# Moving row additions, output copies and evictions by gaps between matrix products

## The chip, the core and the metric

The kernel runs on one core of one Trainium2 chip. The metric is the device time of one execution in microseconds (us); the comparison is by the median of several runs. The profile is of one execution of its own, so its span and its time differ a little from that median.

The engines that matter here are PE (matrix products), ACT and DVE (elementwise work), POOL (which in this kernel only issues DMAs) and SP (which only issues DMAs too). The program gives each of them one instruction stream.

## The reference, cut to what matters

Two results are computed from the same tokens (2048 of 576 values) and mixed by a gate for each token.

```python
def _A_ref(x, w_r, w_i):
    X = rfft2(x); X = X * (w_r + 1j * w_i); return irfft2(X, s=(S, D))
def _B_ref(x, w_gate, w_up, w_down):
    h = gelu(x @ w_gate) * (x @ w_up)          # 576 -> 4608, twice
    return h @ w_down                          # 4608 -> 576
g = sigmoid((x * gate_w).sum(-1, keepdims=True))
return g * _A_ref(x) + (1 - g) * _B_ref(x)
```

All data is float32. The products are made accurate by splitting each operand into a high and a low part and adding three products.

## The kernel before, in words

**The products set the frame.** After a short opening, the program goes through 34 blocks in `products(b, k)`, k from 0 to 33. A block makes seven combined products of gate and up (a Strassen scheme; the loop over n from 0 to 6) for 1024 tokens and two of the hidden tiles. Each of the seven has two halves, each half is one call of `seven` with seven matrix products of 512 columns. Between them stand the down products: `down` makes one with twelve products of 288 columns, which add up in one of two PSUM buffers `pdn`. A block has eight of them: three after n = 1, three after n = 4 and two after n = 6. The last block has two after each of the first five and `finale` makes the last eight in another way.

**The gap is the unit of order.** Nothing is scheduled by hand in time. Each `seven` and each `down` ends in one call of `gap`. A gap counts up `count[0]`, runs all functions that `at(n, fn)` has put off to this count (in the order of their due count, equal ones in the order in which they were put off), then runs the work of `post`, and gives the rest of its room to one generator of other work (`gens[0]`), which computes the spectral half. Note that `at(1, fn)` before a `gap` puts `fn` into that very gap, behind whatever was due there already. The program only fixes the order of each engine's stream; at run time engines wait by semaphores.

**Credit.** Each product adds its length times 1.08 to `credit[0]`; each DVE operation takes its cost from it. The generator runs while the credit is positive. What is carried over is held to `cap[0]`: 2.0, and 3.0 in the column stage. A generator that yields nothing ends its turn for this gap. A second generator in `side` runs beside it.

**The spectral half** goes forward over the rows, through the column stage (`columns`, 16 column products on PE from `product`, operands loaded by POOL), and back over the rows in two halves h = 0 and h = 1 (`inverse_rows(h)`). For h = 0 the last part is, in this order: `fetch(2)` loads a quarter from the DRAM array `home` into `tmp`; `adds` scales eight finished rows, each into one of five places (three in `wtb`, two in `low`), by DVE and ACT in turn, and two gaps later has POOL add it to `yd[u]` in DRAM by an accumulating DMA; `spin` (a butterfly of ten DVE operations) and `settle` (copies on ACT and DVE back to `rows`) treat the fetched quarter; then the last quarter is fetched into `tmp` (index 0 of `places_of`), and after seven gaps spun and settled. Index 1 of `places_of` means `wtb` and `low` in place of `tmp`. For h = 1 `adds` takes the row whose down product was put some eleven gaps ago (`added`).

**The down results.** `down` hands the finished PSUM buffer to ACT (line 1007: scaled by `omg` into one of four tiles `stg`), and `put` lets POOL add `stg` to `yd[u]` by an accumulating DMA (line 989). For the blocks 13, 14, 16 and 17 of the first 1024 tokens `put` stores to DRAM tiles `ye` instead; 32 later DMAs (line 1476) add these to `yd[0..7]`. In the column stage the eviction goes to `post`; outside of it is issued at once, ahead of the gap. ACT's other work in gaps is the gelu of a block's hidden tiles (line 1421, put off by `finish`), copies of high parts, and copies of finished PSUM tiles (`pgu`, `px`, `xraw`, line 236), which the next products wait for.

**The outputs.** `yd[0..7]` is copied from DRAM to `y` by eight SP DMAs ahead of the last block (line 1638); `yd[8..15]` is finished in `finale`.

Of the kernel before, what the change touches and what calls it, by code (L numbers as in the profile page):

```python
# [13 lines left out]
ALU = mybir.AluOpType  # L14
# [3 lines left out]
D = 576  # L18
# [142 lines left out]
def _build(nc, tc, a):  # L161
    with ExitStack() as ctx:
# [3 lines left out]
        vec, act, pl, pe = nc.vector, nc.scalar, nc.gpsimd, nc.tensor  # L166
# [123 lines left out]
        def columns():  # L290
# [126 lines left out]
            yield from step()  # L417
            side.append(beside())
            ops["ahead"] = True
            cap[0] = 3.0  # L420
            for kb in range(16):
                was, more = kb > 0, kb + 1 < 16
                v = product(0, kb, xh, xl)
# [163 lines left out]
        def along(main, beside):  # L587
            side.append(beside)
            yield from main
            yield None  # L590
            for c in side.pop():
                yield c

        def waits(n):
            for _ in range(n):
                yield None
# [61 lines left out]
        def fetch(e, q=None):  # L658
            for x, i, j in places_of(e if q is None else q)[1]:
                nc.sync.dma_start(x, home[:, SW * (4 * e + i):SW * (4 * e + j)])  # L660

        def inverse_rows(h):
            sp = zb[0][:, 1664:1664 + SW]

            def spin(e, q):
                yield from butterfly_of(places_of(q)[0], range(4), 1, sp)

            def pad():
                vec.memset(rows.rearrange("p (c k) -> p c k", c=2)[:, :, 8 * KF:], 0.0)

            def settle(e, q):
                T = places_of(q)[0]
                yield from moved(lambda t, c: (spread(c, t), two(T[t % 4])[:, c, 0:KF]), range(4 * (e % 2), 4 * (e % 2) + 4))

            if h == 0:
                yield from waits(1)
                yield from spin(0, 0)
                pad()
                yield from along(settle(0, 0), spin(1, 1))
                yield from settle(1, 1)  # L680
            else:
                pad()
            yield from inverse_stages()
            places = [wtb[:, D * i:D * (i + 1)] for i in range(3)] + [free_low[:, D * i:D * (i + 1)] for i in range(2)]
            if h == 0:
                fetch(2)
                yield from adds(0, range(4), places)
                yield from along(adds(0, range(4, 8), places), spin(2, 0))
                yield from settle(2, 0)
                at(1, lambda: fetch(3, 0))  # L690
                yield from waits(7)
                yield from spin(3, 0)
                yield from settle(3, 0)
            else:
                yield from adds(1, range(8), places + [tmp[:, D * i:D * (i + 1)] for i in range(4)])
                yield from waits(3)
            ops["half"] = h + 1

        def adds(h, ts, places):
            R = rows.rearrange("p (k t) -> p t k", t=8)  # L700
            todo_t = list(ts)
            n = count[0]
            while todo_t:
                if count[0] >= n:
                    t = min(todo_t, key=lambda t: abs(count[0] - added[8 * h + t] - 11)) if h else todo_t[0]
                    todo_t.remove(t)
                    u = 8 * h + t
                    o = places.pop(0)
                    places.append(o)
                    if h == 0 and t % 2:  # L710
                        act.activation(o, R[:, t, 0:D], AF.Copy, scale=gs[:, u:u + 1])
                    else:
                        vec.tensor_scalar(o, R[:, t, 0:D], gs[:, u:u + 1], None, op0=ALU.mult)
                    at(2, lambda u=u, o=o: pl.dma_start(yd[u], o, accum_op=ALU.add))  # L714
                    n = count[0] + (1 + len(todo_t) % 2 if h else 1)
                    yield 0.8
                else:
                    yield None
# [51 lines left out]
        def at(n, fn):  # L770

            if n == 0:
                fn()
                return
            later.append((count[0] + n, fn))
            later.sort(key=lambda x: x[0])
# [214 lines left out]
        def down(prev, t):  # L991

            p, i, tb = prev[:3]
            u = 8 * p + 4 * tb + t
            v = ps_dn()
            for part in range(2):
                down_mm((v[:, 0, 0:HD], v[:, 1, 0:HD]), prev, t, part)
            if t == 3:
                for _, hold, _ in prev[3]:
                    h = hold[0]  # L1000
                    if any(h is x for x in base + extra):
                        free_h.append(h)
            if p == 0 and i == 0 and tb == 0:
                copy(held(u).rearrange("p (c k) -> p c k", c=2), v[:, :, 0:HD])
            else:
                assert ops.get('released', 0) > min(dnn[0], 3)
                out = lambda: put(u, lambda o: act.activation(o.rearrange("p (c k) -> p c k", c=2), v[:, :, 0:HD], AF.Copy,  # L1007
                                                              scale=omg[:, u:u + 1]), i == 0, i)
                if ops.get("ahead"):
                    post.append(out)  # L1010
                else:
                    out()
            behind[0] = t % 2 == 0
            gap()
            behind[0] = False
# [382 lines left out]
        def products(b, k):  # L1398
# [41 lines left out]
            for n, (name, nd) in enumerate(zip(("a11", "a12", "s2", "s3", "s1", "a22", "s4"), downs)):  # L1440
                m = n + 3
                b.prep(k + m // 7, m % 7)
                if n == 0 and k:
                    b.load_d(k)
                if n == 4:
                    w, x = dns[:, j % 4:j % 4 + 2], b.both
                    copy(w[:, :, 0], x)

                    def rest_of(w=w, x=x):
                        vec.tensor_tensor(w[:, :, 1], x, f(w[:, :, 0]), ALU.subtract)  # L1450
                        credit[0] -= 1.35

                    seq(("dn", j), (5, rest_of))
                if n == 3 and opening:
                    b.more()
                if n == 0:
                    b.load(k + 1, "r11", "r21")
                elif n == 3:
                    b.load(k + 1, "r22")
                elif n == 4:  # L1460
                    b.load(k + 1, "r12")
                if n == 4:
                    fore = [ps_x(s) for s in range(2)] if k % 2 else [ps_gu() for _ in range(2)]
                ps = acc if n in (2, 3, 5) else fore
                for s in range(2):
                    soon = opening and n in (0, 2)
                    b.seven(ps[s], k, n, name, s, n in (0, 4), (lambda n=n, s=s: copy((acc, None, u)[n][s], ps[s])) if soon else None)
                    if n in (0, 2, 3) and not soon:
                        copy((acc, None, u, u3)[n][s], ps[s])
                    elif n in (4, 6):  # L1470
                        at(0 if end else 1, lambda x=(u3, u)[n // 2 - 2][s], y=ps[s]: add(x, y))
                if turn:
                    ops["turn"] = True
                    if n == 6:
                        for q, e in enumerate(ye):
                            at(60 + 6 * q, lambda e=e: pl.dma_start(yd[e[1]], ye[e], accum_op=ALU.add, max_dma_last_dim=D))
                    assert ops["kept"]
                    at(2, lambda name=name: swap(name))
                if n in (1, 4, 5, 6):
                    finish(*{1: ("c11", fore, gl[0]), 4: ("c22", u3, u3[0]), 5: ("c21", acc, gl[1]), 6: ("c12", u, u[0])}[n])  # L1480
                if not (opening or end):
                    nd = (n + 1 + n // 6 if ops.get("ahead") else (0, 3, 3, 3, 6, 6, 8)[n]) - popped
                    popped += max(0, nd)
                for _ in range(nd):
                    if pend:
                        down(*pend.pop(0))
                if end and n == 5:
                    while gens:
                        credit[0] = 1.0
                        gap()  # L1490
                    load_last(1)
# [142 lines left out]
        for k in range(len(b.groups)):  # L1634
            if k == len(b.groups) - 1:
                assert ops["half"]
                for u in range(8):
                    nc.sync.dma_start(a["y"][u], yd[u])
            products(b, k)
        finale(pend)  # L1640

# [61 lines left out]
```

## Time and profile before

| what | before |
|---|---|
| median of 3 runs (lowest to highest) | 1334.81 us (1332.42 to 1335.05) |
| the profiled execution: time | 1332.48 us |
| the profiled execution: span, first to last instruction | 1330.7 us |
| DVE, ACT, POOL busy | 1137.7, 831.4, 308.4 us |
| mean granted clock of TensorE | 0.996 |

The span is 1.78 us shorter than the execution's time; that rest lies outside of the instructions. PE is the busiest engine by far, so the reading starts from the moments in which it is idle. An engine's busy time is no measure of what it costs: only where PE waits for it does it lengthen the run.

### The profile page before, as it was taken

What the parts mean: (1) busy time and instruction counts of PE and PEld (TensorE: products, weight loads), DVE (VectorE), ACT (ScalarE), POOL (GpSimd) and SP (SyncE); (2) the same over time, 40 slices, a digit from 0 to 9 for tenths busy, and PEclk for the clock granted to TensorE, in tenths of its full rate; (3) what the DMA queues carried; (4) which work ended last, traced back from release to release, by engine and by line L of the source; (5) the groups of instructions that cost most, each with busy time, mean ns of one, the idle gap of its engine ahead of it and who ended that gap; (6) DMA issues with size and microseconds to landing.
All of it is one profiled execution on the core that took longest, in us unless ns stands there. A gap on an engine that the chain in (4) does not pass through costs nothing.

```text
span 1330.7 us, 20521 instructions
## 1 busy us (share of the span) xinstructions
PE 1305.1 (98%) x7210; PEld 1153.0 (87%) x7210; DVE 1137.7 (85%) x1734; ACT 831.4 (62%) x1405; POOL 308.4 (23%) x392
## 2 busy tenths in 40 slices
PE   9999999999999999999999999999999979999998
PEld 7888888888888888888888888887888868888888
DVE  7898999878999988778898798679999868999844
ACT  5665655666565667768787878666555556564542
POOL 0011221112222111124310343322332332221241
PEclk9999999999999999999999999999999989999999
DMA  9779999797776799879966999999999997667898
GB/s 349 242 204 227 261 268 245 167 284 134 148 142 142 170 315 363 266 187 306 366 210 206 244 236 221 248 192 168 175 172 167 204 176 166 140 141 141 154 239 208
DMA packets 202391, 285.93 MB, mean 215 GB/s; under 512 B 18160, under 2 KB 118640, under 8 KB 201392
## 3 DMA queue, kind: packets, MB, share of 16 engines
q0 software_dynamic: 64848, 110.13, 48.0%
q1 hardware_dynamic: 137008, 174.06, 40.1%
q8 instruction: 56, 0.92, 0.3%
q10 hardware_dynamic: 432, 0.44, 0.1%
q14 instruction: 47, 0.39, 0.1%
HBM read 157.87 MB, written 137.88 MB: 222 GB/s over the span
## 4 chain that ended last, share of the span: by engine, by line
PE 71%; issue 13%; DVE 4%; DMA 4%; POOL 4%; ACT 4%; SPq 0%; POOLq 0%; DVEq 0%; ACTq 0%
PE pdn L974 25%; PE pgu L1389 17%; PE px L1389 17%; PE pgu L1391 3%; POOL yd L989 3%; PE px L1391 3%; DMA yd<-stg 2%; PE pdn L351 1%; POOL yd L714 1%; DMA gub<-wd 1%; ACT stg L1007 1%; DMA rows<-away 1%; DVE rows L266 1%; DMA home<-rows 1%; PE px L910 1%
## 5 line engine op out<-in xcount | busy, mean ns | idle before, releaser
L1007 ACT ACTIVATE stg<-pdn,omg 128x576 f32<-128x576 f32 x276 | 204.7, 742 | 311.8 <-PE pdn L974 228.3
L989 POOL DMA_DIRECT2D yd<-stg x232 | 202.4, 879 | 799.2 <-ACT stg L1007 764.8
L974 PE MATMUL pdn<-dn,hb 128*128 128x288 f32 x1356 | 197.7, 294 | 1.2 <-ACT stg L1007 1.2
L974 PEld LDWEIGHTS pdn<-dn,hb 128*128 128x128 f32 x1356 | 189.4, 188 | 8.3 <-ACT stg L1007 2.5
L1389 PE MATMUL pgu<-xhi,gub 128*128 128x512 f32 x480 | 148.7, 391 | 0.0
L1389 PE MATMUL pgu<-til,gub 128*128 128x512 f32 x516 | 133.8, 395 | 8.9 <-ACT xraw L236 8.9
L974 PE MATMUL pdn<-dn,ext 128*128 128x288 f32 x816 | 130.8, 295 | 0.0
L974 PE MATMUL pdn<-dn,gub 128*128 128x288 f32 x816 | 129.7, 294 | 0.0
L236 ACT ACTIVATE gub<-low 128x512 fp32r<-128x512 f32 (+1 forms) x163 | 100.9, 621 | 41.4 <-DVE low L1361 34.7
L974 PEld LDWEIGHTS pdn<-dn,ext 128*128 128x128 f32 x816 | 119.3, 188 | 4.1
L1389 PEld LDWEIGHTS pgu<-til,gub 128*128 128x128 f32 x516 | 97.0, 191 | 29.4 <-ACT xraw L236 9.8
L1376 DVE TENSOR_TENSOR gub<-low,gub 128x512 fp32r<-128x512 f32 x151 | 103.3, 684 | 15.1 <-ACT gub L236 15.1
L974 PEld LDWEIGHTS pdn<-dn,gub 128*128 128x128 f32 x816 | 115.6, 188 | 0.0
L1389 PE MATMUL px<-xhi,gub 128*128 128x512 f32 x344 | 107.5, 394 | 6.0 <-ACT pgu L236 5.2
L1389 PEld LDWEIGHTS pgu<-xhi,gub 128*128 128x128 f32 x480 | 87.7, 188 | 16.0
L1389 PE MATMUL px<-til,gub 128*128 128x512 f32 x396 | 101.1, 391 | 0.3 <-ACT xraw L236 0.3
L1389 PE MATMUL pgu<-xlo,gub 128*128 128x512 f32 x240 | 93.5, 390 | 0.0
L1389 PEld LDWEIGHTS px<-til,gub 128*128 128x128 f32 x396 | 73.0, 188 | 14.9 <-ACT xraw L236 0.7
L1389 PEld LDWEIGHTS px<-xhi,gub 128*128 128x128 f32 x344 | 62.5, 188 | 21.1 <-ACT pgu L236 8.5
L974 PE MATMUL pdn<-dn,hx 128*128 128x288 f32 x444 | 70.3, 294 | 0.0
L1361 DVE TENSOR_TENSOR low<-low 128x512 f32<-128x512 f32 x98 | 67.2, 685 | 0.9
L1391 PE MATMUL pgu<-til,gub 128*128 128x512 f32 x172 | 67.3, 391 | 0.0
(309 smaller groups left out, 2765.2 us busy)
## 6 DMA issues: line engine op xcount, KB each, us to landing
yd<-stg POOLq DMA_DIRECT2D x232, 288.0 KB, 5.6
low<-ws SPq DMA_DIRECT2D x114, 256.0 KB, 5.3
gub<-tails SPq DMA_DIRECT2D x179, 128.0 KB, 4.5
gub<-wd SPq DMA_DIRECT2D x68, 288.0 KB, 5.5
tails<-wtb SPq DMA_DIRECT2D x28, 448.0 KB, 5.8
ye<-stg POOLq DMA_DIRECT2D x32, 288.0 KB, 5.6
yd<-ye POOLq DMA_DIRECT2D x32, 288.0 KB, 8.5
slot<-tails SPq DMA_DIRECT2D x59, 128.0 KB, 4.5
```

The lines of the kernel that those rows point to most:

```text
L236: act.activation(o, i, AF.Copy)
L266: vec.tensor_tensor(o, p, q, op)
L351: pe.matmul(v[:, al, :NK], cc[d][2 * al + q], two(x)[:, al], start=n == 0, stop=n == 2)
L714: at(2, lambda u=u, o=o: pl.dma_start(yd[u], o, accum_op=ALU.add))
L910: pe.matmul(ps[j][s], w[:, l, k, cs[s]], x0k, start=k == 0 and l == 0 and x is xhi, stop=k == 3 and x is xlo)
L974: pe.matmul(ps[half], h[:, l, c], d[:, q, half * HD:(half + 1) * HD], start=part == 0 and n == 0, stop=part == 1 and n == 2)
L989: pl.dma_start(yd[u], o, accum_op=ALU.add)
L1007: out = lambda: put(u, lambda o: act.activation(o.rearrange("p (c k) -> p c k", c=2), v[:, :, 0:HD], AF.Copy, scale=omg[:, u:u + 1]), i == ...
L1361: vec.tensor_tensor(o, p, q, ALU.subtract)
L1376: vec.tensor_tensor(v[:, 0:5:4], x, f(v[:, 1:4:2]), ALU.subtract)
L1389: pe.matmul(ps, l, x[:, t], start=first and t == 0 and q == 0, stop=False, skip_group_check=True)
L1391: pe.matmul(ps, w[:, 512 + P * s:512 + P * (s + 1)], xt, start=False, stop=True, skip_group_check=True)
```

## The change

It has six parts. (1) In the column stage the carried credit is held to 2.4 and not 3.0. (2) After the first row additions the last quarter of h = 0 is fetched four gaps on into `wtb` and `low` instead of after `settle` into `tmp`, and `spin` follows four gaps after `settle`, not seven. (3) `adds` takes a row every second gap in both halves (before: every gap for h = 0, one or two for h = 1). (4) Outside the column stage `down` puts the eviction off by `at(1, out)`. (5) The 32 DMAs from `ye` start 44 gaps after the turn, 5 apart, instead of 60 and 6. (6) The eight copies to `y` are issued from 4 gaps after h = 0 is finished, one every 4 gaps, and no longer ahead of the last block.

```diff
@@ columns
-            cap[0] = 3.0
+            cap[0] = 2.4
@@ inverse_rows
                 yield from along(adds(0, range(4, 8), places), spin(2, 0))
+                at(4, lambda: fetch(3, 1))
                 yield from settle(2, 0)
-                at(1, lambda: fetch(3, 0))
-                yield from waits(7)
-                yield from spin(3, 0)
-                yield from settle(3, 0)
+                yield from waits(4)
+                yield from spin(3, 1)
+                yield from settle(3, 1)
+                for u in range(8):
+                    at(4 + 4 * u, lambda u=u: nc.sync.dma_start(a["y"][u], yd[u]))
@@ adds
-                    n = count[0] + (1 + len(todo_t) % 2 if h else 1)
+                    n = count[0] + 2
@@ down
                 if ops.get("ahead"):
                     post.append(out)
                 else:
-                    out()
+                    at(1, out)
@@ products
-                            at(60 + 6 * q, lambda e=e: pl.dma_start(yd[e[1]], ye[e], accum_op=ALU.add, max_dma_last_dim=D))
+                            at(44 + 5 * q, lambda e=e: pl.dma_start(yd[e[1]], ye[e], accum_op=ALU.add, max_dma_last_dim=D))
@@ the loop over the blocks
             if k == len(b.groups) - 1:
                 assert ops["half"]
-                for u in range(8):
-                    nc.sync.dma_start(a["y"][u], yd[u])
             products(b, k)
```

## The prediction, made before the changed kernel was run

> **What bounds the kernel now.** I read the page's busy times first, then PE's waits, then the timeline and stretches around the longest one.
>
> ```profile
> span 1330.7 us, 20521 instructions
> PE 1305.1 (98%) x7210; PEld 1153.0 (87%) x7210; DVE 1137.7 (85%) x1734; ACT 831.4 (62%) x1405; POOL 308.4 (23%) x392
> ...
> PE pgu L1389 <- ACT xraw L236: 8.9, 2, 7.9
> PE px L1389 <- ACT pgu L236: 5.2, 6, 1.6
> PE pgu L1389 <- ACT px L236: 2.1, 2, 1.6
> ...
> PE pdn L974 <- ACT stg L1007: 1.2, 2, 0.8
> ```
>
> PE is busy for 1305.1 of 1330.7 us; 25.6 us are all that a change of order can win, plus what a lowered clock costs. One wait alone holds 7.9 us. The other waits for ACT are at most 1.6 us each. The timeline shows what lies before the long one:
>
> ```profile
> 1056.67 0.85 DVE L713 TENSOR_SCALAR wtb<-rows,gs 128x576 f32<-128x576 f32 x1
> ...
> 1057.83 1.70 POOL L714 DMA_DIRECT2D yd<-wtb  x1
> ...
> 1068.95 1.33 ACT L711 ACTIVATE wtb<-rows,gs 128x576 f32<-128x576 f32 x1 [3.05 <-DMA yd<-wtb]
> ...
> 1075.02 1.34 ACT L711 ACTIVATE wtb<-rows,gs 128x576 f32<-128x576 f32 x1 [4.11 <-DMA yd<-wtb]
> ...
> 1076.27 0.58 ACT L236 ACTIVATE xraw<-pgu 128x512 f32<-128x512 f32 x1
> ...
> 1076.90 2.93 PE L1389 MATMUL pgu<-til,gub 128*128 128x512 f32 x6 [7.87 <-ACT xraw L236]
> ```
>
> These are the row additions of h = 0. ACT wants a place in `wtb` again while the DMA that empties it is in flight; it waits 3.05 and 4.11 us, the copy of a finished PSUM tile stands behind it in ACT's stream, and PE waits 7.87 us for that copy. The stretches around it show what follows:
>
> ```profile
> 1058.00:1069.00 11.00, 11.00 (x64) 9.62 (x62) 4.13 (x7) 6.16 (x9) 4.45 (x6) 1.00 1.12 241
> 1069.00:1076.90 7.90, 0.04 (x1) 0.00 (x0) 5.04 (x8) 3.79 (x5) 5.56 (x7) 0.65 1.10 186
> 1076.90:1082.40 5.50, 5.50 (x15) 4.35 (x16) 4.25 (x8) 2.59 (x5) 0.67 (x1) 0.57 1.10 196
> 1082.40:1100.00 17.60, 17.60 (x104) 15.92 (x103) 12.11 (x18) 9.96 (x16) 2.94 (x4) 1.00 0.75 172
> ```
>
> The last three columns are granted clock, DMA share and GB/s. After the stall PE runs at a clock of 0.57 for 5.50 us, which loses 5.50 x 0.43 = 2.37 us. So this place costs 7.87 + 2.37 = 10.24 us, and the DMA engines are full (shares of 1.10 to 1.12) throughout.
>
> **Row additions (3) and the fetch (2).** A gap's length comes from the chain of waits:
>
> ```profile
> 121.62 4.77 PE pdn L974 x36
> ...
> DMA to landing us min/median/max: 6.5/7.6/11.0
> ...
> L1476 POOL DMA_DIRECT2D yd<-ye x32: 1028/1342/1637, 739.8 to 1056.5; - x32
> ```
>
> Three down products take 4.77 us, so a gap is 1.59 us. The second row is the landing of the eight additions of h = 0. Before, each of the five places is wanted again after four gaps (both calls of `adds` share a gap at their seam), and the DMA is issued two gaps after the row: two gaps, 3.2 us, are left for a landing of 6.5 to 11.0. Afterwards the same place is wanted eight gaps after it was filled, six after its issue: 9.5 us. At the median of 7.6 nothing waits; at 11.0 ACT waits 1.5 us, less than its earlier 3.05. The landing should shorten too: the last `ye` addition was issued at 1056.5, into this very crowd; 31 intervals of six gaps took 316.7 us, 1.70 us a gap, so with part 5 they begin at 739.8 - 16 x 1.70 = 712.6 and end 155 x 1.70 later, at 976. I cost the addition's wait at nothing: -7.87, and -2.37 for the clock. If this cover fails, see the second rival.
>
> [...]
>
> What is late next is the fetch. The additions end some six gaps later than before, but most of `spin` runs beside them, the fetch no longer waits for `settle`, and three gaps of waiting are gone; I count h = 0 finished within two gaps of before. The fetch now needs `wtb` and `low`, whose last addition is issued about three gaps ahead of it; so it sits in SP's queue until that lands, and `spin` comes four or five gaps after.
>
> ```profile
> L660 SPq EVENT_SEMAPHORE  x2: 17/2767/5517, 1052.6 to 1086.1; - x2
> L660 SPq DMA_DIRECT2D tmp<-home x2: 319/323/327, 1054.3 to 1092.7; - x2
> ...
> DMA to landing us min/median/max: 7.8/8.1/8.3
> ...
> 895.54 0.74 DVE L571 TENSOR_TENSOR rows<-tmp,gub 128x289 f32<-128x289 f32 x1 [3.78 <-DMA slot<-tails]
> ...
> 915.44 0.73 PE L1389 MATMUL px<-xhi,gub 128*128 128x512 f32 x2 [1.61 <-ACT pgu L236]
> ```
>
> A fetch lands in 8.1 us. Held 3 to 5 us on SP, with the weight loads of the block behind it, it lands 2 to 6 us after DVE wants it, and DVE's products of the hidden tiles and low parts queue behind that first operation. SP was held 5.5 us here before (first row) and no PE wait followed within 20 us of it. A DVE wait of 3.78 us was followed by a PE wait of 1.61 us 20 us later, which may be unrelated. Bounds 0 and +2.4; I take +0.8.
>
> For h = 1 the additions take 14 gaps, not 11, and so end three gaps later, well before the last block empties the generators. With two gaps each I count every row picked at least seven gaps after its last put. Before, the last was picked two gaps after it, and this is what followed:
>
> ```profile
> POOL yd L714 <- DMA yd<-stg: 8.9, 1, 8.9
> ...
> ACT stg L1007 <- DMA yd<-stg: 10.4, 4, 3.7
> ...
> 1297.75 3.46 PE L974 MATMUL pdn<-dn,hb 128*128 128x288 f32 x24 [0.36 <-ACT stg L1007]
> ```
>
> POOL stood 8.9 us, four evictions waited 10.4 us, but two PSUM buffers hid all but 0.36 us from PE. I take -0.4.
>
> **Output copies (6).** They leave a stage in which SP is held for 7.2 us and enter one that has room:
>
> ```profile
> 1269.13 7.18 SPq L1638 DMA_DIRECT2D y<-yd  x8
> ...
> 1125.00:1150.00 25.00, 25.00 (x138) 22.07 (x138) 24.86 (x31) 13.32 (x23) 5.95 (x7) 1.00 0.82 158
> 1150.00:1175.00 25.00, 25.00 (x137) 22.01 (x136) 24.86 (x32) 13.44 (x23) 4.23 (x5) 1.00 0.74 149
> ```
>
> Eight copies of 288 KB every 6.4 us meet a DMA share of 0.74 to 0.82 and PE that waits for nothing. Each costs SP under 1 us. I take 0; their cover is that weights come some three products ahead; without it each copy could cost up to its own issue, 8 x 0.9 = 7.2 us.
>
> **Evictions (4).** `at(1, out)` runs in the gap that follows at once, so the copy isn't later by a product; it only moves behind what was due in that gap. In gaps after a down product that is a gelu on ACT, three a block.
>
> ```profile
> L1007 ACT ACTIVATE stg<-pdn,omg 128x576 f32<-128x576 f32 x276 | 204.7, 742 | 311.8 <-PE pdn L974 228.3
> ...
> ACT stg L1007 <- PE pdn L974: 228.3, 157, 4.3
> ...
> ACT xraw L1421 <- DVE xraw L1434: 2.6, 2, 1.7
> ...
> DVE gl L1417 <- ACT gl L1421: 14.1, 10, 3.7
> ...
> L1421 ACT ACTIVATE xraw<-xraw 128x512 f32<-128x512 f32 x68 | 42.4, 623 | 2.6 <-DVE xraw L1434 2.6
> ```
>
> ACT idles ahead of 157 evictions, 1.45 us on average; a gelu of 0.62 us fits into that and DVE, which waited 14.1 us for gelus of one kind, gets them earlier. Bounds: all 7.3 us of PE's waits for `pgu` and `px` copies gone, or the third rival. I take -0.5.
>
> **Column stage (1, 5).** The trace shows neither a smaller cap nor the five `ye` additions that move into it (16 gaps and 1 in 6 earlier). PE's waits there:
>
> ```profile
> 622.56 0.40 PE L351 MATMUL pdn<-tmp 128*128 128x290 f32 x1 [1.26 <-DVE tmp L431]
> 638.57 1.85 PE L974 MATMUL pdn<-dn,hb 128*128 128x288 f32 x12 [0.85 <-ACT stg L1007]
> 772.66 1.65 PE L1389 MATMUL pgu<-til,gub 128*128 128x512 f32 x6 [1.02 <-ACT xraw L236]
> 781.66 0.79 PE L351 MATMUL pdn<-tmp,xtl 128*128 128x290 f32 x4 [0.34 <-DVE tmp L455]
> ```
>
> Together 3.47 us: less burst work could save all of it, and later operands could cost as much again. I take 0. A lower cap can stretch this stage by some gaps, which PE fills with products; it matters only if the generators outlast the last block's sixth product, some 16 gaps of slack.
>
> **The sum.** -7.87 - 2.37 + 0.8 - 0.4 - 0.5 = -10.3 us. The profiled execution took 1332.48 us, so 1322.1; it lies 2.3 us under the median of 1334.81, from which the same sum gives 1324.5. I predict 1323.
>
> **Rivals.** *More is won:* earlier gelus and a quieter DMA remove most of the waits of at most 1.6 us ahead of blocks as well, 4 to 8 us more, 1315 to 1319. For it: DVE's 14.1 us of waits. Against: at several of these ACT is busy without a break, and order makes no work less. 0.20.
>
> *The stall comes back smaller:* landings stay at 11 us and the fetch holds DVE, so 3 to 6 us of PE idle and clock remain: 1326 to 1330. For it: six gaps against 11.0 us. 0.14. [...]
>
> *Nothing is won on balance:* the shifted stages meet the blocks elsewhere, and the eight waits of 0.2 to 1.6 us for `pgu` and `px` copies (7.3 us) double, with the fetch at its bound: 1331 to 1335. 0.10.
>
> *Slower:* the gelus delay evictions. Place: the two runs of three down products in each of the 25 blocks outside the column stage, 50 runs; the third product needs the first one's buffer 1.59 us after its end, the eviction takes 0.74, so an ACT that comes over 0.85 us late stalls PE. If a gelu's 0.62 us fell into PE's time in half of them or more, that is 15 to 31 us: 1337 to 1353. Against it: PE waited for `stg` evictions just 1.2 us in all. 0.10.
>
> **How the numbers follow.** Forecast (1319 to 1326) 0.46, more 0.20, smaller 0.14, nothing 0.10, slower 0.10. A measurement can tell some 0.2%, 2.7 us. Faster 0.80, same 0.10, slower 0.10. The range of 1315 to 1330 leaves out the last two.
>
> **What would show it.** Right: no PE wait over 2 us between 1056 and 1085, no clock under 1.00 there, no `yd<-ye` DMA after 980, additions 3.2 us apart. The fetch: a DVE wait of 2 to 6 us near 1095. Evictions: DVE's waits for line 1421 shrink, PE's for `stg` stay near 1 us. Wrong would be a new PE wait of several us at the additions, at the fetch, or over many small waits at down products.

## The result, and the profile after

The changed kernel took 1319.0 us (median of 4 runs, 1317.98 to 1320.34) beside 1334.6 us for the kernel before; the ratio is 0.9887 with a 95% interval of 0.987 to 0.9904. By the medians it is 15.6 us faster. The experiments ran in three later jobs, in which the kernel before had medians of 1332.3 to 1332.8, so they are compared by ratio.

In the changed kernel the numbers of the lines behind the change are higher by two: the eviction is line 1009, the gelu 1423, the issue of an addition 716. Its page, and below it PE's waits:

```profile
span 1318.6 us, 20529 instructions
PE 1303.7 (99%) x7210; PEld 1154.6 (88%) x7210; DVE 1136.2 (86%) x1734; ACT 836.5 (63%) x1405; POOL 308.3 (23%) x392
```

```profile
PE pdn L976 <- ACT stg L1009: 4.6, 2, 2.3
PE px L1391 <- ACT pgu L236: 2.4, 3, 1.6
...
PE pdn L351 <- DVE tmp L455: 1.1, 1, 1.1
PE pgu L1391 <- ACT xraw L236: 0.9, 1, 0.9
```

The wait of 7.87 us is gone altogether. The list holds something new at its head instead: two waits of 2.3 us each for an eviction. Where they lie is seen in the stretches of both kernels (length, then busy time of PE, PEld, DVE, ACT and POOL with counts, then clock, DMA share and GB/s). Before:

```profile
560.00:700.00 140.00, 137.86 (x780) 122.54 (x779) 115.84 (x186) 108.23 (x184) 40.87 (x71) 1.00 0.85 262
700.00:860.00 160.00, 158.63 (x899) 140.97 (x898) 127.65 (x204) 121.74 (x205) 48.26 (x61) 1.00 0.97 228
860.00:980.00 120.00, 115.46 (x632) 100.74 (x631) 109.55 (x150) 69.73 (x113) 34.15 (x37) 1.00 0.94 178
1050.00:1100.00 50.00, 42.13 (x226) 37.02 (x225) 32.31 (x51) 26.30 (x40) 16.64 (x18) 0.90 0.98 212
```

After:

```profile
560.00:700.00 140.00, 140.00 (x799) 125.28 (x798) 113.19 (x181) 107.55 (x183) 41.17 (x70) 1.00 0.85 264
700.00:860.00 160.00, 154.16 (x854) 136.80 (x853) 126.89 (x204) 120.26 (x202) 52.23 (x66) 0.98 1.03 228
860.00:980.00 120.00, 118.33 (x654) 103.97 (x653) 107.14 (x149) 70.59 (x115) 38.27 (x41) 1.00 1.02 193
1050.00:1100.00 50.00, 50.00 (x287) 44.84 (x286) 39.08 (x63) 33.18 (x51) 17.95 (x20) 1.00 1.01 233
```

In the last row PE now finishes 287 matmuls in the 50 us in which it finished 226. But in the second row it does 854 instead of 899, at a clock of 0.98: the second half of the column stage became slower, and the change won in spite of it.

In the profile the ends of matmuls are modelled, so that PE's busy time can cover short pauses and a lowered clock (before, PE counted as busy for all of the 5.50 us from 1076.90 on, at a clock of 0.57). So I also counted lost time from start to start: for each matmul the distance to the next one, less the median distance of its kind (0.227 us for 512 columns, 0.132 for 288), summed by stage. For the kernel before this gives 34.3 us where the idle time was 25.6. The table gives it in us, for the two kernels and for four of the experiments told below:

| stage, us | before | after | part 3 alone | parts 3 and 4 | without 4 | without 1 |
|---|---|---|---|---|---|---|
| 0 to 275 | 3.1 | 3.3 | 3.3 | 3.1 | 3.3 | 3.8 |
| 275 to 560 | 4.8 | 2.8 | 4.8 | 2.8 | 4.8 | 3.1 |
| 560 to 700 | 3.4 | 0.5 | 3.4 | 3.4 | 0.6 | 3.4 |
| 700 to 860 | 2.9 | 10.7 | 2.2 | 2.6 | 9.8 | 2.3 |
| 860 to 980 | 6.3 | 3.0 | 7.0 | 7.4 | 4.1 | 8.7 |
| 980 to 1050 | 2.0 | 1.4 | 2.0 | 1.5 | 1.4 | 1.5 |
| 1050 to 1100 | 10.5 | 0.1 | 0.1 | 0.1 | 0.1 | 0.2 |
| 1100 to the last matmul | 1.3 | 0.6 | 0.6 | 0.6 | 0.7 | 0.8 |
| sum | 34.3 | 22.2 | 23.3 | 21.4 | 24.8 | 23.7 |

The difference of the first two sums, 12.1 us, is the difference of the spans (1330.7 and 1318.6). Of it, 10.3 us come from the row additions, 2.0 from the forward stage, 3.0 from 560 to 700, 3.4 from 860 to 980 and 1.2 from the rest; 7.8 are given back between 700 and 860 (all taken before rounding).

The medians differ by more than the spans, because the profiled execution of the kernel before (1332.48 us) was at the low end of its runs and that of the changed kernel (1320.34 us) was the slowest of its four. The 10.7 us between 700 and 860 also hold two falls of the clock of 1.7 us each, which the last section tells. Executions with the same waits and without the falls lost 7.6 us there (part 5 undone) and 7.5 (part 6 undone).

### The profile page after: what moved, and what is told of

It reads as the page before. It is cut to its first block, busy times and chain, and to the rows that moved or that the text cites. A ratio compares the mean times of both kernels' runs of the same rounds, so it can differ in the third digit from the quotient of the medians.

```text
span 1318.6 us, 20529 instructions
## 1 busy us (share of the span) xinstructions
PE 1303.7 (99%) x7210; PEld 1154.6 (88%) x7210; DVE 1136.2 (86%) x1734; ACT 836.5 (63%) x1405; POOL 308.3 (23%) x392
## 4 chain that ended last, share of the span: by engine, by line
PE 90%; DVE 4%; ACT 4%; issue 1%; DMA 1%; DVEq 0%; ACTq 0%; SPq 0%
PE pdn L976 32%; PE pgu L1391 22%; PE px L1391 22%; PE pgu L1393 4%; PE px L1393 4%; PE pdn L351 1%; PE px L912 1%; ACT stg L1009 1%; DVE xraw L1436 0%; PE pgu L912 0%; DMA away<-wtb 0%; ACT tmp L737 0%; ACT low L251 0%; PE pgu L892 0%; PE pgu L893 0%
## 5 line engine op out<-in xcount | busy, mean ns | idle before, releaser
L1391 PE MATMUL pgu<-til,gub 128*128 128x512 f32 x516 | 131.6, 390 | 0.9 <-ACT xraw L236 0.9
L1391 PE MATMUL px<-xlo,gub 128*128 128x512 f32 x172 | 67.6, 393 | 0.0
```

The lines of the kernel that those rows point to most:

```text
L1391: pe.matmul(ps, l, x[:, t], start=first and t == 0 and q == 0, stop=False, skip_group_check=True)
```

## The experiments

**Part 3 alone, without and with the early fetch.** The first experiment took parts 2 and 3 into the kernel before, the second part 3 alone.

```diff
-                    n = count[0] + (1 + len(todo_t) % 2 if h else 1)
+                    n = count[0] + 2
...
+                at(4, lambda: fetch(3, 1))
                 yield from settle(2, 0)
-                at(1, lambda: fetch(3, 0))
-                yield from waits(7)
-                yield from spin(3, 0)
-                yield from settle(3, 0)
+                yield from waits(4)
+                yield from spin(3, 1)
+                yield from settle(3, 1)
```

> The kernel before with the row additions two gaps apart and the last quarter fetched early into wtb and low (parts 2 and 3 alone). Theory A, the places were wanted too soon: PE's 7.87 us wait and the half clock behind it go, the time falls by 10 us to about 1324, and the rest of the trace stays as before. Rival B, the ye additions crowded the DMA engines and spacing alone is not enough: with the ye additions still running until 1056, a wait of ACT for yd<-wtb of 2 us or more and a PE wait of several us remain, time 1328 or more.

Measured: 1326.36 us, ratio 0.9961 (0.9945 to 0.9977), and ten runs spread from 1322.9 to 1332.5. The stall at 1069 was gone (0.1 us lost from 1050 to 1100), but 6.5 us were lost from 1100 to 1240 in the profiled execution, which took 1330.43. Of this experiment the SP queue's waits, then DVE's timeline, then PE's:

```profile
SPq L660 <- DMA yd<-wtb: 7.8, 1, 7.8
```

```profile
1094.58 0.68 DVE L959 TENSOR_TENSOR ext<-gl,ext 128x512 fp32r<-128x512 f32 x1
1101.95 0.77 DVE L94 TENSOR_TENSOR gub<-wtb 128x580 f32<-128x580 f32 x1 [6.69 <-DMA wtb<-home]
```

```profile
1108.54 1.66 PE L1389 MATMUL px<-til,slot 128*128 128x512 f32 x6 [1.60 <-ACT xraw L236]
1112.70 2.80 PE L1389 MATMUL px<-til,slot 128*128 128x512 f32 x6 [2.28 <-ACT xraw L236]
```

The fetch stood 7.8 us on SP until the last addition had left `wtb`, DVE stood 6.7 us for the fetch, and PE waited twice for ACT copies that came late behind it. This execution lay 4 us above the median of its kernel, and it also lost 5.7 us between 700 and 860 (2.9 before); the cause of that stays open. Theory A was right on the stall but had nothing else change; rival B's PE wait for the additions did not come, though ACT still stood 1.2 us and DVE 3.6 us for a place. To separate the two, the next one dropped the early fetch.

> The kernel before with the row additions two gaps apart and nothing else (part 3 alone; the last quarter is fetched into tmp after settle, as before). Theory A, what the first experiment lacked was lost to the early fetch, which held SP for 7.8 us behind the last addition and DVE for 6.7 us: without it the PE waits at 1106 to 1112 go, and the full 10 us of the stall are won, 1322 to 1324 by the median of before then shown less 10. Rival B, the loss at 1106 comes from the additions themselves reaching further into the next block: PE still loses 4 to 6 us between 1090 and 1130, and the time is like the first experiment's 1326.

Measured: 1322.98 us, ratio 0.9924 (0.9905 to 0.9943), 9.8 us less than the 1332.82 before in the same job. The two intervals do not meet. The stretches of this run:

```profile
1050.00:1100.00 50.00, 50.00 (x284) 44.70 (x284) 38.04 (x61) 32.64 (x51) 17.69 (x20) 1.00 1.08 256
1100.00:1240.00 140.00, 140.00 (x778) 124.41 (x777) 134.67 (x192) 79.73 (x136) 27.14 (x32) 1.00 0.72 142
```

PE is busy throughout both. Theory A holds: spacing the additions by one more gap wins the 10 us by itself, with the `ye` additions as late as before and the DMA engines no less full (1.08 from 1050 to 1100, 0.98 before), and the early fetch costs time in that kernel: 3.9 us between the gains of the two medians, 9.8 and 5.9.

**The changed kernel with one part undone.** Four experiments undo parts 4, 1, 5 and 2 one at a time, a fifth part 6.

```diff
-                    at(1, out)
+                    out()
```

> The changed kernel with the evictions issued at once again (part 4 undone). Theory A, the order behind the gelu frees DVE and shortens the waits ahead of blocks: PE's losses between 275 and 560 us go back from 2.8 to about 4.8 us, DVE waits again some 14 us for gelus, and the time rises by 2 to 5 us to 1321 to 1324. Rival B, the order is without effect and the shorter waits come from the shifted stages: the time stays at 1319 and DVE's waits for gelus rise without a cost to PE.

Measured: 1322.54 us, ratio 0.9927 (0.991 to 0.9945), slower than the changed kernel's 0.9887 (0.987 to 0.9904). From 275 to 560 us it lost 4.8 us again. DVE's waits for gelus, first in the changed kernel, then with part 4 undone:

```profile
DVE gl L1419 <- ACT gl L1423: 1.5, 1, 1.5
```

```profile
DVE gl L1419 <- ACT gl L1423: 12.2, 10, 2.8
DVE xraw L1419 <- ACT xraw L1423: 8.0, 10, 2.2
```

Theory A holds: the gelu now runs while ACT would wait for the down product, DVE is freed of some 19 us of waiting, and PE's waits ahead of blocks become shorter. By the sums of the table this is worth 2.6 us of lost PE time, although the changed kernel's sum holds one fall of the clock (1.7 us) more.

```diff
-            cap[0] = 2.4
+            cap[0] = 3.0
```

> The changed kernel with the carried credit of the column stage at 3.0 again (part 1 undone). Theory A, the smaller credit shifts the column steps so that an eviction stands behind a copy that waits for DVE: PE's two waits of 2.3 us at 752 and 795 and the half clock after each go, PE's loss between 700 and 860 us falls from 10.7 to about 3, some of the 3 us won between 560 and 700 is lost again, and the time is 1312 to 1317. Rival B, the ye additions moved into this stage cause the two waits: they stay, and the time is 1319 or more.

Measured: 1320.63 us, ratio 0.9913 (0.9894 to 0.9931), not told apart from the changed kernel. The stretches of this run:

```profile
700.00:860.00 160.00, 159.14 (x907) 141.99 (x906) 129.55 (x207) 121.39 (x205) 54.23 (x67) 1.00 1.04 240
860.00:980.00 120.00, 114.50 (x614) 99.66 (x613) 108.38 (x149) 68.33 (x111) 37.08 (x40) 0.99 0.96 179
```

The two 2.3 us waits are gone and 8.4 us are won back between 700 and 860, as theory A said. But from 560 to 700 2.9 us are lost, as it also said, and from 860 to 980 another 5.7, which it did not: there PE did 614 matmuls instead of 654. The time missed its 1312 to 1317. The smaller credit moves losses from one stage to another.

```diff
-at(44 + 5 * q, lambda e=e: pl.dma_start(yd[e[1]], ye[e], ...))
+at(60 + 6 * q, lambda e=e: pl.dma_start(yd[e[1]], ye[e], ...))
```

> The changed kernel with the ye additions 60 gaps after the turn and 6 apart again (part 5 undone). Theory A, they are not in the chain of the two waits in the column stage and the row additions have room without it: 1318 to 1321, both 2.3 us waits stay. Rival B, the ye additions cause the two waits: these go and the time falls to about 1312. Rival C, the row additions need them gone: an ACT wait for yd<-wtb of 2 us or more comes back near 1060, and the time rises by 3 us or more.

Measured: 1319.93 us, ratio 0.991 (0.9891 to 0.9929). Both waits of 2.3 us stayed and no wait of ACT or DVE for `yd<-wtb` came back; SP's fetch stood 1.9 us for it. Theory A holds.

For part 2 undone (the `+` and `-` lines of the fetch in the first diff exchanged):

> The changed kernel with the last quarter fetched into tmp after settle, seven gaps ahead of its spin (part 2 undone). Theory A, the early fetch into wtb and low wins nothing by itself, since the generators have slack at the end: 1318 to 1320, no new PE wait. Rival B, it is needed to finish the spectral half in time: the row additions of h = 1 slide into the last block and the time rises by 2 us or more.

Measured: 1319.33 us, ratio 0.9897 (0.9878 to 0.9916). Theory A holds for the time, though not to the letter for PE: it waited five times for a copy of `pgu` in place of three (3.1 us beside 2.4), and 1.6 us were lost from 1100 to 1240 (0.3 in the changed kernel). For part 6 undone (the copies in front of the last block):

> The changed kernel with the eight copies to y issued ahead of the last block again (part 6 undone). Theory A, the last block has room: PE loses at most 1 us more after 1240 us, time 1318 to 1321. Rival B, the copies slow the landing of the last accumulating DMAs, evictions wait for their tiles, and PE loses 2 us or more in the last block.

Measured: 1317.37 us, ratio 0.9887 (0.9866 to 0.9909). ACT's waits in the last 80 us of this run held this row, and PE none for an eviction:

```profile
ACT stg L1007 <- DMA yd<-stg: 7.4, 5, 2.7
```

So evictions do wait longer with the copies there, as rival B says, but with two PSUM buffers none of it reaches PE; theory A holds, at a time 0.6 us under its range.

**Parts 3 and 4 alone.**

> The kernel before with parts 3 and 4 alone (row additions two gaps apart, evictions by one gap outside the column stage). Theory A, these two carry nearly the whole change and add up: 10 us and 3 us less than before, a ratio of 0.989 to 0.992, and the shorter waits between 275 and 560 us (2.8 in place of 4.8). Rival B, the smaller credit of part 1 carries the rest: the ratio stays near the 0.992 of part 3 alone.

Measured: 1319.12 us, ratio 0.9892 (0.987 to 0.9914). Theory A holds: two of the six parts give what all six give, within the interval. By the table their lost time is even 0.8 us less.

**The two new waits.** Their timeline in the changed kernel, ACT and DVE beside PE:

```profile
749.90 0.46 DVE L433 TENSOR_TENSOR wtb<-rows,wtb 128x290 f32<-128x290 f32 x1
...
750.45 0.69 ACT L250 ACTIVATE wtb<-wtb 64x580 f32<-64x580 f32 x1 [2.76 <-DVE wtb L433]
...
751.15 0.69 ACT L251 ACTIVATE wtb<-wtb 64x580 f32<-64x580 f32 x1
...
751.86 0.74 ACT L1009 ACTIVATE stg<-pdn,omg 128x576 f32<-128x576 f32 x1
...
752.65 1.06 PE L976 MATMUL pdn<-dn,hb 128*128 128x288 f32 x6 [2.31 <-ACT stg L1009]
```

In the column stage evictions go to `post`, behind the generator's work of the gap. Here that work is two copies which wait 2.76 us for DVE; the eviction stands behind them, and the down product after the next needs its buffer. The smaller credit moves the column steps against the blocks, and two such meetings arise. Two experiments issued evictions earlier in this stage: the first all of them, the second only where a second down product follows.

```diff
-                if ops.get("ahead"):
-                    post.append(out)
-                else:
-                    at(1, out)
+                at(1, out)
```

> The changed kernel with evictions put off by one gap in the column stage too, ahead of the generator's work in that gap instead of behind it. Theory A, the two 2.3 us waits at 752 and 795 us are evictions that stand on ACT behind a copy waiting for DVE: both go with the half clock behind them, PE's loss between 700 and 860 us falls from 10.7 to 3 to 5 us, time 1311 to 1315. Rival B, the column steps on ACT come later by an eviction each and the column products wait instead (PE waits of line 351 for DVE): the loss in this stage stays or grows, 1318 or more.

Measured: 1321.13 us, ratio 0.9908 (0.9887 to 0.993). PE's waits of this run:

```profile
PE pdn L976 <- ACT stg L1009: 2.5, 3, 0.9
...
PE pdn L351 <- DVE tmp L455: 2.3, 3, 1.7
PE pgu L1388 <- ACT xraw L236: 2.3, 4, 0.9
```

Both waits are gone, and more small ones have come: 3.1 us were lost from 560 to 700 (0.5 in the changed kernel) and 9.4 from 700 to 860. Rival B holds.

```diff
-        def down(prev, t):
+        def down(prev, t, soon=False):
...
-                if ops.get("ahead"):
+                if ops.get("ahead") and not soon:
...
-                for _ in range(nd):
+                for q in range(nd):
                     if pend:
-                        down(*pend.pop(0))
+                        down(*pend.pop(0), soon=q + 1 < nd)
```

> The changed kernel, with the eviction of a down product in the column stage issued ahead of the generator's work where the next product on PE is a down product too, and behind it elsewhere as before. Theory A, the two 2.3 us waits arise only there, where the third product needs the buffer and the eviction stands on ACT behind a copy that waits for DVE: both go, the small waits that came when all evictions went ahead do not come, PE's loss between 700 and 860 us falls from 7.5 to 10.7 to 3 to 5 us, and the time falls by 4 to 6 us to about 1314. Rival B, the column steps delayed by these evictions make PE wait at the column products instead: no change, 1318 or more.

Measured: 1318.33 us, ratio 0.9888 (0.9868 to 0.9909). Again both waits are gone, and waits of 0.3 to 1.1 us took their place: 1.6 and 8.0 us lost in the two stretches, where it should have been 3 to 5 in the second. The kernel with part 6 undone has both waits, no fall of the clock and 7.5 us lost in that stretch, so removing the two waits alone won nothing there. My theory named the mechanism of the two waits, but not what bounds this stage; I take rival B as the better account and have no run that shows each of the small waits' causes.

> The same with the eight copies to y issued ahead of the last block as in the kernel before (part 6 undone). Theory A, where the copies stand costs PE nothing: within 1.5 us of the run before it in this job. Rival B, their earlier place takes DMA time from the weight loads: 2 us faster with them back at the end.

Measured: 1318.13 us, ratio 0.989 (0.987 to 0.9911), the same as its neighbour. No version beat the changed kernel by more than the intervals can tell.

## Why the prediction was right, and where it was not

The range of 1315 to 1330 held the time, and the direction was right. The forecast of 1323 was 4 us too high; the evictions' term, some 3 us too small, and the fetch's +0.8 are about as much.

- **Row additions, -7.87 and -2.37.** Right, in mechanism and size: 10.3 us by the table, and part 3 alone won 9.8. The additions stood 2.8 us apart on average where I had 3.2. The shorter landing that I counted on beside it mattered little, though: landings took 7.7 us at the median in the changed kernel and 8.2 with the `ye` additions late again (part 5 undone), and in neither did ACT or DVE wait for a place. With part 3 alone they took 9.3, and only a wait of DVE for a place remained, 2.4 us, at no cost to PE. Six gaps between issue and reuse were enough by themselves.
- **Fetch, +0.8.** In the changed kernel it cost nothing; the last addition held it on SP for 0.9 us. The danger was real and larger than its bound of 2.4: 7.8 us on SP, 6.7 us on DVE and 6.5 us of lost PE time where parts 2 and 3 stood alone. In the changed kernel parts 1, 4, 5 and 6 stand beside it. With any one of these undone SP was held for 1.1 to 4.2 us and DVE for at most 1.2, so no single one of them is needed; how much each does was not separated.
- **Last block, -0.4.** Right: 0.94 us lost from 1240 us on before, 0.25 after.
- **Output copies, 0.** Right.
- **Evictions, -0.5.** The mechanism was right, gelus that run in ACT's waits; the term was mis-sized. It measured 2.6 us by the traces and 3.5 us between the medians, which are of two jobs; between part 3 alone and parts 3 and 4, also of two jobs, the medians differ by 3.9. I had seen DVE's 14.1 us of waits for one kind of gelu and taken a small part of the 7.3 us it might free; the other kind (11.7 us) I left out.
- **Column stage, 0.** This is the step that failed. I bounded it by the waits that were there (3.47 us either way), and the stage lost 7.8 us between 700 and 860 (3.4 of them by the clock) while 3.0 were won from 560 to 700 and 3.4 from 860 to 980. A smaller credit moved every column step against the blocks, and a wait that the trace of before did not hold arose twice. That the sum came out near 0 all the same (with the credit undone 1.5 us are lost by the table) is the cancellation of larger terms: the 0 was luck.
- **The second rival's clock.** This rival left 3 to 6 us of PE idle and clock at the row additions; 0.1 us were lost there. In the column stage, where no term allowed for the clock, some waits of 2.3 us also cost 1.7 us of clock; see the last section.

## What to carry to other kernels

When a ring of buffers is emptied by DMAs, count the time between issue and reuse against the slowest landing in that stage, not in the kernel: one more gap between two additions was worth 10 us here, two thirds of a change with six parts. Put work whose inputs are ready ahead of an instruction that is known to wait on the same engine; outside the column stage it cost nothing here and freed DVE of some 19 us of waiting. And where a parameter shifts one stream of work against another, read every stage of the profile and not only the sum: gains and losses of 3 to 8 us cancelled here.

## What the runs showed of the hardware that was not expected

Waits of 2.3 us were followed by a fall of the granted clock, but not each time. The same two waits stand in the changed kernel and in four of the experiments. In the stretches of the changed kernel the clock fell at both:

```profile
748.00:762.00 14.00, 11.69 (x61) 10.19 (x61) 10.15 (x18) 7.77 (x13) 3.97 (x5) 0.88 1.16 260
788.00:802.00 14.00, 11.70 (x59) 10.40 (x59) 13.76 (x24) 7.64 (x14) 5.01 (x7) 0.88 1.16 257
```

With the `ye` additions late again it fell at neither, with PE idle just as long:

```profile
748.00:762.00 14.00, 11.69 (x72) 10.47 (x71) 11.43 (x21) 9.07 (x16) 4.07 (x6) 1.00 1.12 260
788.00:802.00 14.00, 11.70 (x69) 10.42 (x68) 13.79 (x24) 8.71 (x15) 4.18 (x6) 1.00 1.06 247
```

Over five profiled executions with two such waits each, it fell 4 times in 10 (2 of 2 in the changed kernel, 1 of 2 with part 4 and with part 2 undone, none with part 5 and with part 6 undone). By the rows of the changed kernel each fall takes 14 x 0.12 = 1.7 us. The clock's own record in the trace of the changed kernel has half clock from 754.11 to 757.52 us and from 795.07 to 798.48, 3.41 us each time. The first begins 1.46 us after its wait ended (at 752.65), the second 0.15 us before its wait ended (at 795.22); of the 3.41 us ahead of each PE was idle for 1.96 and 2.15 us. At the 7.87 us wait before, the record has 10.24 us at half clock, which begin 2.3 us after the wait does and end 4.7 us after it.

So the length of a wait did not tell by itself whether the clock fell: of ten waits of 2.3 us, at the same two places of the program, four cost 1.7 us of clock each and six none. What decided between them these runs do not show. Waits of up to 1.63 us in the changed kernel, and of up to 1.61 us in the kernel before, left the clock at 1.00.
